# Eight one-bank PSUM tiles in place of four two-bank tiles, in a fused attention and mixer kernel

## The chip, the cores and the metric

The kernel runs on one core of one Trainium2 chip. The metric is the device time of one execution in microseconds (us); of several runs the median counts. A core has TensorE (PE, matrix products; its weight loads are the rows PEld), VectorE (DVE), ScalarE (ACT), GpSimd (POOL) and SyncE (SP, which here issues most DMAs). PE writes its results to PSUM, a memory of eight banks; a bank holds 512 float32 numbers in each of 128 partitions. DVE and ACT read the results from there.

## The reference

The shapes are B=8, H=8, S=576, D=64, so C=H*D=512; the token layer is 256 wide, the channel layer 1536.

```python
cum = np.cumsum(np.log(np.clip(f, 0.0001, 1.0)), axis=-1)
scores = q @ k.T / 8 + cum[..., :, None] - cum[..., None, :]
scores = np.where(causal, -1e9, scores)
attn = softmax(scores)                  # + 1e-9 in the denominator
x = (attn @ v) as (B, S, H*D)
u = x + (np.maximum(x.T @ w_tok1, 0) @ w_tok2).T
out = u + np.maximum(u @ w_ch1, 0) @ w_ch2
```

## The kernel before

The 64 heads of attention are worked in 32 pairs, four to each of the eight batch images. The two heads of a pair (s = 0 and 1) sit on the two halves of PE's rows. Products keep float32 accuracy by splitting an operand into a high and a low part, so that most products are three matmuls: high by high, high by low, low by high.

For a pair, the steps are these. POOL splits q and k (`hl`, L729 and L510). PE makes the scores of five row tiles t = 0 to 4, 64 to 576 columns wide because the mask is causal (`score`, L765). DVE adds the mask, writes the sum to SBUF (`pr`) and takes the minimum of each row, all in one custom instruction, followed by a short one that reads the minimum out into `nmin` (`rmin`, L775). ACT takes the exponential (`expo`, L779). DVE sums and inverts the denominators (L799, L802), and POOL scales (`norm`, L807). PE transposes the probabilities in three groups (`trs`, L825), two banks each; ACT copies the high part to `pt` (L504) and DVE subtracts for the low part (L513). PE multiplies with v (L870, and L858 for the low parts of the last piece), and ACT and DVE carry the result to `xt` (L885, L889). When an image is done, `mixer` runs on it piece by piece among the next pairs: transposes (L1353), products with the token weights and with the first 256 of the 1536 channels (`joint`, L1336), and what carries them out of PSUM (L504, L513, L516, L1416, L1465). That is the attention stage, up to 736 us. From 776 us a second stage runs the rest of the channel layer (L1152 to L1219), with weights that come by DMA.

The order of the work isn't that of the loops. The loops only create operations (`p.op(engine, duration, function, rd=..., wr=..., bufs=...)`). The class `Plan` then gives them out by the table `ORDER`, which holds for every engine the numbers of its operations in the order in which they are issued, and assigns each `Buf` a slot, among them the eight PSUM banks b0 to b7. The plan treats each bank as a resource of its own. In the program, however, PSUM is declared as four tiles `unit0` to `unit3` of 1024 columns (L1536), and a bank is the half of one (L1538): b0 and b1 are unit0, b2 and b3 unit1, b4 and b5 unit2, b6 and b7 unit3. The waits between the engines are set when the program is built, from the tiles that its instructions read and write.

The only buffer that uses a whole unit is the widest score tile, t = 4: 576 columns, as 288 and 288 columns on both sides of the bank border, read by one minimum of 576 columns. Its slot is of the kind "un" (L1477), a pair of banks. The other four score tiles of a head share two banks.

Of the kernel before, what the change touches and what calls it, by code (L numbers as in the profile page):

```python
# [9 lines left out]
F32 = mybir.dt.float32  # L10
F32R = mybir.dt.float32r
# [7 lines left out]
    FILL=36, F1=2, FQ=4, n_raw=1, n_vr=1, n_hl=1, n_vv=2, n_pr=2, n_pt=4, n_xn=1,  # L19
# [46 lines left out]
    ),  # L66
    DVE=(
# [390 lines left out]
def build(nc, env, dims):  # L458
# [261 lines left out]
    for n2 in range(HB // 2):  # L720
# [60 lines left out]
        for ts in ((4,), (3, 0), (2, 1)):  # L781
# [4 lines left out]
            for s in (0, 1):  # L786
                sm = (2 * n2 + s) % 4
                for t in ts:
                    p.op("DVE", d_dve(end[t]), lambda t=t, s=s, sm=sm, f=rmin: f(t, s, sm), rd=[ps[s]], wr=[(pr, s, t), ("nmin", sm, t)], bufs=[ps[s], pr])
# [914 lines left out]
```

## Time and profile before

| | |
|---|---|
| median of 3 runs | 1294.0 us (1290.93 to 1298.85) |
| the profiled execution, its own time | 1291.14 us |
| its span in the trace | 1289.4 us |
| PE busy | 1080.4 us, 84% of the span, 10030 matmuls |
| DVE busy | 862.2 us, 67%, 2093 instructions |
| ACT busy | 637.2 us, 49%, 1582 instructions |
| POOL busy | 440.2 us, 34%, 519 instructions |
| mean granted clock of PE | 0.939 of full speed |

Busy time is time in which an engine executes; the rest of the span it waits or issues. "Idle before" of an instruction is the time that its engine stood still just ahead of it, and the releaser is the instruction that ended last among those it waited for. A matmul's duration depends on the clock that PE is granted.

### The profile page before, as it was taken

Reading aid. Unit: us, or ns where it says so; the run is one execution under the profiler, and the core shown is the slowest. Engines: PE = TensorE matmul, PEld = TensorE weight load, DVE = VectorE, ACT = ScalarE, POOL = GpSimd, SP = SyncE. Lnnn points to the kernel's source line nnn. Section 1 sums busy time; section 2 is a strip of 40 time slices with the busy share of each in tenths; the row PEclk is TensorE's granted clock in tenths of the full one; section 3 lists DMA queues with packets and bytes.
Section 4 is the critical chain, followed back from the end, with each engine's and each line's share of the span. In section 5 each row is a group of like instructions: output and inputs, shape, how many; then the busy total and the mean of one; then the engine's idle time right before and its main releaser. Section 6 shows DMA issues by size and latency. Waiting matters only on the chain.

```text
span 1289.4 us, 26886 instructions
## 1 busy us (share of the span) xinstructions
PE 1080.4 (84%) x10030; PEld 935.8 (73%) x10030; DVE 862.2 (67%) x2093; ACT 637.2 (49%) x1582; POOL 440.2 (34%) x519
## 2 busy tenths in 40 slices
PE   6777887878877777778778779899999999899897
PEld 4566777877767677767667667778787787688776
DVE  7788565666464465465465687886797696588376
ACT  5577575666564556566566544333252252143132
POOL 6665546466454374465355200000211101110110
PEclk8678997999988989999999979999999999999999
DMA  6221221121312112121222257898979888877774
GB/s 196 86 61 56 70 75 51 48 97 33 117 42 93 60 62 84 29 75 38 74 84 73 73 190 259 264 312 258 314 233 303 265 249 276 267 239 216 263 233 155
DMA packets 125858, 192.77 MB, mean 150 GB/s; under 512 B 18976, under 2 KB 77088, under 8 KB 124704
## 3 DMA queue, kind: packets, MB, share of 16 engines
q1 hardware_dynamic: 125632, 190.91, 46.3%
q8 instruction: 79, 1.29, 0.4%
q14 instruction: 51, 0.42, 0.1%
q10 hardware_dynamic: 96, 0.15, 0.0%
HBM read 144.34 MB, written 46.66 MB: 148 GB/s over the span
## 4 chain that ended last, share of the span: by engine, by line
PE 46%; DVE 11%; ACT 7%; issue 4%; DMA 2%; SPq 0%; POOL 0%; DVEq 0%; ACTq 0%; POOLq 0%
PE unit L1336 8%; PE unit L1217 4%; PE unit L1219 4%; PE unit L1152 4%; PE unit L1218 4%; PE unit L1154 4%; PE unit L1153 4%; PE unit L870 3%; PE unit L765 3%; ACT pt L504 2%; DVE pt L513 2%; PE unit L825 1%; DVE xt L889 1%; DVE pr L775 1%; ACT pr L779 1%
## 5 line engine op out<-in xcount | busy, mean ns | idle before, releaser
L807 POOL TENSOR_SCALAR pr<-pr,rec 128x320 f32<-128x320 f32 (+4 forms) x320 | 166.8, 539 | 188.8 <-DVE rec L802 135.9
L779 ACT ACTIVATE pr<-pr,nmin 128x320 f32<-128x320 f32 (+4 forms) x320 | 177.2, 558 | 42.8 <-DVE nmin L775 42.1
L513 DVE TENSOR_TENSOR pt<-unit,pt 128x512 fp32r<-128x512 f32 x192 | 126.1, 685 | 91.4 <-ACT pt L504 55.1
L775 DVE CUSTOM_DVE_ANT_0 pr<-unit,mask 128x576 f32<-128x576 f32 (+4 forms) x320 | 145.8, 483 | 53.1 <-PE unit L765 19.4
L504 ACT ACTIVATE pt<-unit 128x512 fp32r<-128x512 f32 x192 | 106.0, 598 | 89.2 <-PE unit L1336 35.5
L870 PE MATMUL unit<-pt,vv 64*128 64x512 f32 (+7 forms) x1152 | 131.0, 350 | 22.0 <-DVE pt L513 9.9
L765 PE MATMUL unit<-hl 64*128 64x288 f32 (+4 forms) x1008 | 112.5, 318 | 34.5 <-DVE pt L513 14.1
L870 PEld LDWEIGHTS unit<-pt,vv 64*128 64x128 f32 x1152 | 109.6, 206 | 31.9 <-DVE pt L513 12.0
L765 PEld LDWEIGHTS unit<-hl 64*128 64x128 f32 x1008 | 92.7, 197 | 44.7 <-DVE pt L513 15.8
L825 PE MATMUL unit<-ident,pr 64*128 64x64 f32 x1536 | 74.5, 241 | 43.7 <-DVE nmin L775 15.0
L825 PEld LDWEIGHTS unit<-ident,pr 64*128 64x128 f32 x1536 | 65.0, 152 | 53.8 <-issue 12.8
L889 DVE TENSOR_TENSOR xt<-unit,xt 64x64 f32<-64x64 f32 (+1 forms) x128 | 57.5, 453 | 59.8 <-ACT xt L885 42.6
L885 ACT ACTIVATE xt<-unit 64x64 f32<-64x64 f32 (+1 forms) x128 | 50.6, 404 | 63.1 <-PE unit L870 28.0
L1336 PE MATMUL unit<-t2h,ring 64*128 64x288 f32 x512 | 66.6, 316 | 14.2 <-DVE xt L889 6.0
L765 PE MATMUL unit<-cd,sel 64*128 64x288 f32 (+4 forms) x384 | 77.9, 357 | 0.0
L1336 PE MATMUL unit<-ring,w2h 64*128 64x288 f32 x512 | 67.6, 312 | 12.1 <-DVE ring L516 3.9
L510 POOL TENSOR_TENSOR hl<-raw,hl 128x1152 fp32r<-128x1152 f32 x28 | 74.5, 2662 | 1.8
L1336 PE MATMUL unit<-xn,t1h 64*128 64x256 f32 x512 | 64.4, 321 | 11.0 <-DVE pt L513 5.7
L504 ACT ACTIVATE hid<-h 128x480 fp32r<-128x480 f32 x75 | 45.1, 603 | 54.7 <-PE unit L1218 33.6
L1336 PEld LDWEIGHTS unit<-t2h,ring 64*128 64x128 f32 x512 | 53.8, 198 | 21.4 <-DVE xt L889 8.4
L1170 ACT ACTIVATE h<-unit 128x480 f32<-128x480 f32 x20 | 11.3, 570 | 113.3 <-PE unit L1154 86.6
L1336 PEld LDWEIGHTS unit<-ring,w2h 64*128 64x128 f32 x512 | 53.2, 192 | 18.0 <-ACT ring L504 3.5
(246 smaller groups left out, 3076.7 us busy)
## 6 DMA issues: line engine op xcount, KB each, us to landing
pw<-wd SPq DMA_DIRECT2D x280, 256.0 KB, 3.9
raw<-in_qk SPq DMA_DIRECT2D x28, 576.0 KB, 4.0
d_raw<-in_w_ch SPq DMA_DIRECT2D x80, 128.0 KB, 3.1
ud<-xt SPq DMA_DIRECT2D x8, 1152.0 KB, 5.0
pd<-part SPq DMA_DIRECT2D x32, 288.0 KB, 2.5
wd<-pw SPq DMA_DIRECT2D x20, 384.0 KB, 4.3
vr<-in_v SPq DMA_DIRECT2D x64, 80.0 KB, 2.4
out_t<-d_raw SPq DMA_DIRECT2D x19, 240.0 KB, 3.7
```

Source lines behind the costliest of these rows:

```text
L504: nc.scalar.activation(out, in_, func, scale=scale)
L510: nc.gpsimd.tensor_tensor(out, in_, asf(hi), op=ALU.subtract)
L513: nc.vector.tensor_tensor(out, in_, asf(hi), op=ALU.subtract)
L765: nc.tensor.matmul(at(buf)[:, of : of + w], q, k, start=(x == 0), stop=(x == len(passes)))
L775: nc.vector.tensor_tensor_reduce(prob(t, s), x, y, -1.0 / D**0.5, 3e38, op0=ALU.add, op1=ALU.min, accum_out=E["nmin"][sm][:m, t : t + 1])
L779: nc.scalar.activation(x, x, AF.Exp, bias=E["nmin"][sm][:m, t : t + 1], scale=-1.0, accum_out=E["sums"][sm][:m, t : t + 1])
L807: nc.gpsimd.tensor_scalar(x, x, E["rec"][sm][:m, t // 2, t % 2 : t % 2 + 1], 0.0, op0=ALU.mult, op1=ALU.add)
L825: nc.tensor.transpose(at(ps[s])[:, k * D : (k + 1) * D], at(pr)[r, x, :, :].rearrange("p a b -> p (a b)"), E["ident"][r, r])
L870: nc.tensor.matmul(at(av[s])[:, 512 - w :], at(vv)[r, vblk(j), :], at(pt)[r, z, c : c + w], start=(z, gi, i) == (0, 0, 0), stop=(z, gi, i) ...
L889: "DVE", d_dve(n), lambda ps=ps, o=o, n=n, f=f, xt=xt, me=me, pp=pp: nc.vector.tensor_tensor(at(xt)[me, pp, o : o + n], at(ps)[me, f : f + ...
L1152: nc.tensor.matmul(o, wt[:, 0, :], h_, start=(first and k == 0), stop=False, skip_group_check=True)
L1336: last[s] = nc.tensor.matmul(at(ps[s ^ z])[:, : width[0]], a, m, start=(z == 0 and i == 0), stop=(z == 1 and i == len(todo[s]) - 1), skip_ ...
```

## The change

Four things change.

- PSUM is declared as eight tiles `bank0` to `bank7` of 512 columns.
- The widest score tile is split: columns 0 to 319 (t = 4) lie in one bank and 320 to 575 (t = 5) in another; they are two operations on PE and two minima on DVE. The first minimum goes to a spare column of `nmin`; the second starts from it (`first`) and so yields the minimum of the whole row. The exponential stays one instruction over 576 columns and follows the second minimum.
- `n_hl` goes from 1 to 2, in place of a second slot of `hl` that was laid over the weight buffer `d_raw`; `n_pt` goes from 4 to 3. `nmin` gets one column more.
- `ORDER` is new throughout, for 5357 operations instead of 5261 (32 more on PE, 64 more on DVE). The number of matmuls on PE stays.

```diff
-    FILL=36, F1=2, FQ=4, n_raw=1, n_vr=1, n_hl=1, n_vv=2, n_pr=2, n_pt=4, n_xn=1,
+    FILL=36, F1=2, FQ=4, n_raw=1, n_vr=1, n_hl=2, n_vv=2, n_pr=2, n_pt=3, n_xn=1,
...
-        "10:29 189 194 203 39:2 264 41:2 273 43:3 259 226 231 236 241 371 362 242:2 296 301 306 311:2 432 313 322 357 "
...
         for s in (0, 1):
-            c2, a, bb = Buf("un"), Buf("bk"), Buf("bk")
+            a, bb, c, d = (Buf("bk") for _ in range(4))
             where.append({
...
-                4: (c2, [(512 - HS, 0, HS), (512, HS, HS)]),
+                4: (c, 0, 0, end[2]),
+                5: (d, 0, end[2], end[4] - end[2]),
             })
...
-            nc.vector.tensor_tensor_reduce(prob(t, s), x, y, -1.0 / D**0.5, 3e38, op0=ALU.add, op1=ALU.min, accum_out=E["nmin"][sm][:m, t : t + 1])
+            o = at(pr)[:m, boff[z] + j0 // D : boff[z] + (j0 + w) // D, s, :]
+            first = 3e38 if t < 5 else c0[:m, NS : NS + 1]
+            col = NS if t == 4 else z
+            nc.vector.tensor_tensor_reduce(o, x, y, -1.0 / D**0.5, first, op0=ALU.add, op1=ALU.min, accum_out=c0[:m, col : col + 1])
...
-        for ts in ((4,), (3, 0), (2, 1)):
+        for ts in ((4,), (5,), (3, 0), (2, 1)):
...
-    pairs = [(f"b{2 * i}", f"b{2 * i + 1}") for i in range(4)]
-    k["un"] = pairs[::-1]
...
-    k["hl"].append(tuple(u for s in k["d_raw"] for u in s))
...
-    units = [psum.tile([P, 1024], F32, name=f"unit{i}") for i in range(4)]
-    E["un"] = {(f"b{2 * i}", f"b{2 * i + 1}"): x for i, x in enumerate(units)}
-    bank = {(f"b{i}",): units[i // 2][:, (i % 2) * 512 : (i % 2) * 512 + 512] for i in range(8)}
+    bank = {(f"b{i}",): psum.tile([P, 512], F32, name=f"bank{i}") for i in range(8)}
...
-    for nm, shape in (("nmin", [P, NS]), ("sums", [P, NS + 1]), ("rec", [P, NS // 2 + 1, 4])):
+    for nm, shape in (("nmin", [P, NS + 1]), ("sums", [P, NS + 1]), ("rec", [P, NS // 2 + 1, 4])):
```

The lines of the changed kernel lie 3 to 13 further down: the scores are at L768, the minima at L782, the exponential at L786, the transposes at L838, the copies at L508 and L517, `joint` at L1349.

How the new table moves instructions is shown at three places. A row is line, operation, what it writes <- what it reads, and the shape; in brackets the engines whose semaphores it waits for. The number behind a tile's name tells tiles apart.

The first is PE in the middle of the attention stage, before: the end of the second group of transposes of a pair, the start of the first half of the token layer for the image before, and the start of its second half.

```order
L825 MATMUL unit2_65<-ident_67,pr0_173 128x64
L825 MATMUL unit3_66<-ident_67,pr0_173 128x64
L1336 MATMUL unit1_64<-xn0_181,t1h_102 128x256 [waits DVE_49]
L1336 MATMUL unit3_66<-xn0_181,t1h_102 128x256 [waits DVE_49]
...
L1336 MATMUL unit3_66<-xn0_181,t1h_102 128x256 [waits PE_49,Activation_49]
L1336 MATMUL unit1_64<-xn0_181,t1h_102 128x256 [waits DVE_49]
L1336 MATMUL unit3_66<-xn0_181,t1l_103 128x256
```

The same place in the changed kernel:

```order
L838 MATMUL bank0_63<-ident_71,pr0_178 128x64
L838 MATMUL bank1_64<-ident_71,pr0_178 128x64
L1349 MATMUL bank2_65<-xn0_185,t1h_106 128x256 [waits DVE_49,Activation_49]
L1349 MATMUL bank6_69<-xn0_185,t1h_106 128x256 [waits DVE_49]
...
L1349 MATMUL bank6_69<-xn0_185,t1h_106 128x256 [waits PE_49]
L1349 MATMUL bank2_65<-xn0_185,t1h_106 128x256
L1349 MATMUL bank6_69<-xn0_185,t1l_107 128x256
```

The steps follow each other as before. Before, the transposes and the token layer both wrote halves of unit3; now their tiles have nothing in common, and the second half of the layer begins with no wait for ACT or DVE.

The second place is ACT just behind this, before: the copies of the transposes to `pt` among exponentials of the next pair.

```order
L779 ACTIVATE pr1_174,sums3_84<-pr1_174,nmin3_80 128x7x64
L504 ACTIVATE pt0_177<-unit2_65 128x8x64 [waits DVE_49,PE_49]
L504 ACTIVATE pt1_178<-unit3_66 128x8x64 [waits DVE_49,PE_49,Activation_49]
L779 ACTIVATE pr1_174,sums2_83<-pr1_174,nmin2_79 64x64
L504 ACTIVATE pt0_177<-unit1_64 128x8x64 [waits PE_49]
```

And in the changed kernel:

```order
L786 ACTIVATE pr1_179,sums3_88<-pr1_179,nmin3_84 128x7x64 [waits DVE_49,Activation_49]
L508 ACTIVATE pt0_182<-bank1_64 128x8x64 [waits DVE_49,PE_49,Activation_49]
L786 ACTIVATE pr1_179,sums2_87<-pr1_179,nmin2_83 128x9x64
L508 ACTIVATE pt0_182<-bank0_63 128x8x64 [waits Activation_49]
L508 ACTIVATE pt1_183<-bank7_70 128x8x64 [waits DVE_49,PE_49,Activation_49]
```

The copies come in the same order among the exponentials, but the second copy of a `pt` buffer no longer waits for PE.

The third place is DVE at the minima of the first pair, before:

```order
L775 ISA pr0_173,nmin1_78<-unit2_65,mask_72 128x9x64 [waits PE_49]
L775 ISA nmin1_78 128x1
L775 ISA pr0_173,nmin0_77<-unit3_66,mask_72 128x9x64
L775 ISA nmin0_77 128x1
L775 ISA pr0_173,nmin1_78<-unit0_63,mask_72 128x7x64 [waits PE_49]
```

And in the changed kernel:

```order
L782 ISA pr0_178,nmin0_81<-bank0_63,mask_76 128x5x64 [waits PE_49]
L782 ISA nmin0_81 128x1
L782 ISA pr0_178,nmin1_82<-bank1_64,mask_76 128x5x64 [waits PE_49]
L782 ISA nmin1_82 128x1
L782 ISA pr0_178,nmin0_81<-bank2_65,mask_76,nmin0_81 128x4x64 [waits DVE_49,PE_49]
```

Two pairs of instructions (one for each head, the second instruction of a pair being the read-out) have become four, and the later ones wait for PE and for the read-out before.

## Rows read from the trace of the kernel before

**Rows 1.** Windows: length, busy PE, PEld, DVE, ACT, POOL; PEclk, DMA share, GB/s

```profile
0.00:96.00 96.00, 67.67 (x609) 55.03 (x611) 74.21 (x207) 57.97 (x153) 62.18 (x89) 0.73 0.37 115
96.00:736.00 640.00, 510.39 (x6928) 463.61 (x6925) 375.94 (x1137) 388.84 (x1075) 325.02 (x391) 0.94 0.21 67
736.00:776.00 40.00, 28.71 (x309) 25.82 (x307) 35.35 (x79) 19.74 (x41) 4.56 (x4) 0.83 0.54 176
776.00:1289.00 513.00, 473.65 (x2194) 391.34 (x2193) 376.65 (x673) 170.69 (x314) 48.42 (x36) 0.98 0.81 256
```

**Rows 2.** Two stretches of the attention stage in the same view

```profile
224.00:352.00 128.00, 106.58 (x1549) 98.67 (x1547) 78.20 (x240) 83.44 (x233) 70.92 (x87) 0.99 0.23 74
352.00:480.00 128.00, 98.83 (x1272) 89.14 (x1268) 71.50 (x220) 73.58 (x201) 63.57 (x78) 0.89 0.19 63
```

**Rows 3.** Groups by line, 96 to 736 us: busy, mean ns, idle before, its releasers

```profile
L504 ACT ACTIVATE pt<-unit 128x512 fp32r<-128x512 f32 x174 | 96.1, 598 | 79.6 <-PE unit L1336 35.5 <-PE unit L825 14.6 <-DVE pt L513 11.9
L885 ACT ACTIVATE xt<-unit 64x64 f32<-64x64 f32 (+1 forms) x116 | 45.8, 404 | 54.8 <-PE unit L870 22.1 <-PE unit L1336 14.4 <-PE unit L765 9.8
L513 DVE TENSOR_TENSOR pt<-unit,pt 128x512 fp32r<-128x512 f32 x174 | 114.4, 685 | 84.6 <-ACT pt L504 52.1 <-PE unit L1336 20.9 <-PE unit L858 4.7
L775 DVE CUSTOM_DVE_ANT_0 pr<-unit,mask 128x576 f32<-128x576 f32 (+4 forms) x280 | 127.4, 483 | 47.0 <-PE unit L1336 17.0 <-PE unit L765 16.1 <-PE unit L825 5.0
L889 DVE TENSOR_TENSOR xt<-unit,xt 64x512 f32<-64x512 f32 (+1 forms) x116 | 52.2, 453 | 59.0 <-ACT xt L885 42.0 <-PE unit L1336 9.8 <-PE unit L765 5.8
```

**Rows 4.** Timeline of PE, 381 to 388 us: start, length, instruction, [idle before]

```profile
381.25 1.46 PE L825 MATMUL unit<-ident,pr 64*128 64x64 f32 x32
382.95 0.70 PE L1336 MATMUL unit<-xn,t1h 64*128 64x256 f32 x2 [0.23 <-DVE xn L513]
...
384.81 0.28 PE L1336 MATMUL unit<-ring,t1l 64*128 64x256 f32 x1
...
387.35 0.38 PE L1336 MATMUL unit<-xn,t1h 64*128 64x256 f32 x1 [1.15 <-DVE pt L513]
```

**Rows 5.** Timeline of ACT, the same stretch

```profile
382.70 0.60 ACT L504 ACTIVATE pt<-unit 128x512 fp32r<-128x512 f32 x1 [0.66 <-PE unit L825]
385.17 0.60 ACT L504 ACTIVATE pt<-unit 128x512 fp32r<-128x512 f32 x1 [1.87 <-PE unit L1336]
...
385.99 0.58 ACT L504 ACTIVATE pt<-unit 128x512 fp32r<-128x512 f32 x1
```

**Rows 6.** Timeline of DVE, the same stretch

```profile
383.24 0.36 DVE L775 CUSTOM_DVE_ANT_0 pr<-unit,mask 128x192 f32<-128x192 f32 x1
...
383.52 0.48 DVE L775 CUSTOM_DVE_ANT_0 pr<-unit,mask 128x320 f32<-128x320 f32 x1
...
383.94 0.69 DVE L513 TENSOR_TENSOR pt<-unit,pt 128x512 fp32r<-128x512 f32 x1
...
386.60 0.69 DVE L513 TENSOR_TENSOR pt<-unit,pt 128x512 fp32r<-128x512 f32 x1 [1.58 <-ACT pt L504]
```

**Rows 7.** What PE waited for, 96 to 736 us: total us, times, longest

```profile
PE unit L765 <- DVE pt L513: 14.1, 10, 2.4
PE unit L825 <- DVE nmin L775: 12.4, 14, 1.7
...
PE unit L825 <- POOL hl L729: 1.2, 2, 0.9
```

**Rows 8.** Chain of waits, 96 to 736 us, by line, shares of the whole span

```profile
by line: PE unit L1336 12.8%; PE unit L870 6.8%; PE unit L765 5.3%; ACT pt L504 3.6%; issue 3.3%; DVE pt L513 3.2%; PE unit L825 2.7%; DVE pr L775 2.4%; DVE xt L889 2.3%; ACT pr L779 2.2%; ACT xt L885 2.2%; ACT ring L504 1.4%; DVE xn L513 0
```

**Rows 9.** DVE's groups by shape, 96 to 736 us

```profile
L775 DVE CUSTOM_DVE_ANT_0 pr<-unit,mask 128x576 f32<-128x576 f32 x56 | 41.1, 750 | 3.2 <-PE unit L765 2.4 <-PE unit L858 0.6
L775 DVE CUSTOM_DVE_ANT_0 pr<-unit,mask 128x320 f32<-128x320 f32 x56 | 26.7, 485 | 11.7 <-PE unit L1336 3.9 <-PE unit L825 3.5 <-PE unit L765 2.6
L775 DVE CUSTOM_DVE_ANT_0 pr<-unit,mask 128x192 f32<-128x192 f32 x56 | 19.3, 351 | 4.9 <-PE unit L870 1.8 <-PE unit L1336 1.7 <-PE unit L765 0.7
L775 DVE DVE_READ_ACCUMULATOR2_ANT nmin<- 128x1 f32 x224 | 18.3, 82 | 0.0
```

More of the change, by code (lines that the diff above doesn't have):

```diff
@@ L741, in build @@
         for s in (0, 1):
-            c2, a, bb = Buf("un"), Buf("bk"), Buf("bk")
+            a, bb, c, d = (Buf("bk") for _ in range(4))
             where.append({
-                3: (a, [(0, 0, end[3])]),
-                0: (a, [(end[3], 0, end[0])]),
-                2: (bb, [(0, 0, end[2])]),
-                1: (bb, [(end[2], 0, end[1])]),
-                4: (c2, [(512 - HS, 0, HS), (512, HS, HS)]),
+                3: (a, 0, 0, end[3]),
+                0: (a, end[3], 0, end[0]),
+                2: (bb, 0, 0, end[2]),
+                1: (bb, end[2], 0, end[1]),
+                4: (c, 0, 0, end[2]),
+                5: (d, 0, end[2], end[4] - end[2]),
@@ L749, in build @@
             })
         def score(t, where=where, src=src, fq=fq, n2=n2):
-            i0 = start[t]
-            for g in range(len(where[0][t][1])):
-                passes = ((0, 1),) if fq else ((0, 1), (0, 3), (2, 1))
-                for x in range(len(passes) + 1):
-                    for s in (0, 1):
-                        buf, segs = where[s][t]
-                        of, j0, w = segs[g]
-                        rows = HALF[s]
-                        if x < len(passes):
-                            q, k = (at(src)[rows, y, :] for y in passes[x])
-                            q, k = q[:, i0 : i0 + P], k[:, j0 : j0 + w]
-                        else:
-                            q, k = E["sel"][rows, n2 : n2 + 1].to_broadcast([D, P]), E["cd"][rows, j0 : j0 + w]
-                        nc.tensor.matmul(at(buf)[:, of : of + w], q, k, start=(x == 0), stop=(x == len(passes)))
+            i0 = start[min(t, 4)]
@@ new lines, in score @@
+            passes = ((0, 1),) if fq else ((0, 1), (0, 3), (2, 1))
+            for x in range(len(passes) + 1):
+                for s in (0, 1):
+                    buf, of, j0, w = where[s][t]
+                    rows = HALF[s]
+                    if x < len(passes):
+                        q, k = (at(src)[rows, y, :] for y in passes[x])
+                        q, k = q[:, i0 : i0 + P], k[:, j0 : j0 + w]
+                    else:
+                        q, k = E["sel"][rows, n2 : n2 + 1].to_broadcast([D, P]), E["cd"][rows, j0 : j0 + w]
+                    nc.tensor.matmul(at(buf)[:, of : of + w], q, k, start=(x == 0), stop=(x == len(passes)))
@@ L767, in prob, with rmin @@
         def prob(t, s, pr=pr):
             return at(pr)[: size[t], boff[t] : boff[t] + end[t] // D, s, :]
-        def rmin(t, s, sm, where=where, prob=prob):
-            buf, segs = where[s][t]
-            m, of, w = size[t], segs[0][0], end[t]
-            a = S - P - start[t]
-            x, y = (z.rearrange("p (a b) -> p a b", b=D) for z in (at(buf)[:m, of : of + w], E["mask"][:m, a : a + w]))
-            nc.vector.tensor_tensor_reduce(prob(t, s), x, y, -1.0 / D**0.5, 3e38, op0=ALU.add, op1=ALU.min, accum_out=E["nmin"][sm][:m, t : t + 1])
+        def rmin(t, s, sm, where=where, pr=pr):
+            buf, of, j0, w = where[s][t]
+            z = min(t, 4)
+            m, c0 = size[z], E["nmin"][sm]
+            a = S - P - start[z] + j0
+            x, y = (v.rearrange("p (a b) -> p a b", b=D) for v in (at(buf)[:m, of : of + w], E["mask"][:m, a : a + w]))
+            o = at(pr)[:m, boff[z] + j0 // D : boff[z] + (j0 + w) // D, s, :]
+            first = 3e38 if t < 5 else c0[:m, NS : NS + 1]
+            col = NS if t == 4 else z
+            nc.vector.tensor_tensor_reduce(o, x, y, -1.0 / D**0.5, first, op0=ALU.add, op1=ALU.min, accum_out=c0[:m, col : col + 1])
@@ L779, in expo @@
             nc.scalar.activation(x, x, AF.Exp, bias=E["nmin"][sm][:m, t : t + 1], scale=-1.0, accum_out=E["sums"][sm][:m, t : t + 1])
-        for ts in ((4,), (3, 0), (2, 1)):
+        for ts in ((4,), (5,), (3, 0), (2, 1)):
             ps = [where[s][ts[0]][0] for s in (0, 1)]
-            dur = [hm(w, z) for t in ts for _, _, w in where[0][t][1] for z in ((4, 1) if fq else (1, 1, 1, 1))]
+            dur = [hm(where[0][t][3], z) for t in ts for z in ((4, 1) if fq else (1, 1, 1, 1))]
             rd = [raw, "cd"] if fq else [(hl, 0), (hl, 1), "cd"]
@@ L788, in build @@
                 for t in ts:
-                    p.op("DVE", d_dve(end[t]), lambda t=t, s=s, sm=sm, f=rmin: f(t, s, sm), rd=[ps[s]], wr=[(pr, s, t), ("nmin", sm, t)], bufs=[ps[s], pr])
+                    p.op(
+                        "DVE", d_dve(where[0][t][3]), lambda t=t, s=s, sm=sm, f=rmin: f(t, s, sm), rd=[ps[s]] + ([("nmin", sm, NS)] if t == 5 else []),
+                        wr=[(pr, s, t), ("nmin", sm, NS if t == 4 else min(t, 4))], bufs=[ps[s], pr],
+                    )
                 for t in ts:
+                    if t == 4:
+                        continue
+                    z = min(t, 4)
                     p.op(
-                        "ACT", d_act(end[t], False, 2), lambda t=t, s=s, sm=sm, f=expo: f(t, s, sm),
-                        rd=[("nmin", sm, t)], wr=[(pr, s, t), ("sums", sm, t)], bufs=[pr],
+                        "ACT", d_act(end[z], False, 2), lambda t=z, s=s, sm=sm, f=expo: f(t, s, sm),
+                        rd=[("nmin", sm, z)] + [(pr, s, 4)] * (t == 5), wr=[(pr, s, z), (pr, s, t), ("sums", sm, z)], bufs=[pr],
                     )
@@ L1605, in attn_mixer_kernel @@
         E[kind] = {((kind, i, 0), (kind, i, 1)): x for ((_, i),), x in E[kind].items()}
-    words = raws.rearrange("p i a b -> p (i a b)")[:, : 4 * S].bitcast(F32R)
-    E["hl"][tuple(u for x in E["d_raw"] for u in x)] = words.rearrange("p (k s) -> p k s", s=S)
     E["rr"] = {}
```

453 rows, old and new, of tables (ACT, DVE, PE, POOL) are left out of this document.

## The prediction

> **What bounds the kernel now.** The windows by stage come first [rows 1]. [...] In the steady attention stage (96 to 736 us) no engine is full: PE is busy 510.39 of 640 us at 0.94, ACT 388.84, DVE 375.94, POOL 325.02, and the DMA share is 0.21. Engines wait for each other there. PE's idle time is 640 - 510.4 = 129.6 us, and its work would take 510.4 x 0.94 = 479.8 us at the full clock, so at most 640 - 479.8 = 160.2 us can be won in this stage. It isn't an even loss: from 224 to 352 us PE got 106.58 us of work at 0.99 through in 128 us, which is 0.824 of a full engine, but from 352 to 480 us only 98.83 x 0.89 / 128 = 0.687 [rows 2]. The clock is low where PE was less busy.
>
> Next, what the waits are for [rows 3]. The releaser of an instruction should be the producer of what it reads. A copy to `pt` reads transposes (L825); a copy to `xt` reads products with v (L870, L858); a minimum reads scores (L765). But ACT's copies to `pt` stood 35.5 us for `joint` (L1336), which they do not read, and 14.6 us for the transposes, which they do. Copies to `xt` on ACT: 14.4 + 9.8 us for L1336 and L765, 22.1 us for L870. On DVE, the low parts of `pt`: 20.9 + 4.7 us for L1336 and L858; minima: 17.0 + 5.0 us for L1336 and L825 against 16.1 us for the scores; `xt`: 9.8 + 5.8 us for L1336 and L765. Together 35.5 + 14.4 + 9.8 + 20.9 + 4.7 + 17.0 + 5.0 + 9.8 + 5.8 = 122.9 us for matmuls of other data, against 14.6 + 22.1 + 16.1 = 52.8 us for the right ones: 70% of the time in which these five groups stood released by PE.
>
> The timeline shows how. The transposes of the second group end at 381.25 + 1.46 = 382.71 us [rows 4]. ACT could copy them when its copy of 382.70 is over, at 383.30, but starts at 385.17, released by L1336 [rows 5]. By the order of before the copied bank is in unit3, and the token layer that runs from 382.95 to 384.81 + 0.28 = 385.09 us writes the other bank of unit3: the wait is kept by unit. DVE, after 1.58 us idle, starts its subtraction of a bank of unit1 at 386.60, because ACT's copy ahead of it began only at 385.99 [rows 5, 6]; and PE's next half of the token layer, which writes the other bank of unit1, stands for that subtraction and starts at 387.35 after 1.15 us idle [rows 4]. Each wait has made the next one.
>
> **The change, part by part.**
>
> *One tile for each bank.* All waits on the other bank of a unit go; true ones (a bank to be filled before it is read, and read before it is filled again) stay. What it gives lies between 0 and 160.2 us of the attention stage; a loss can come only from the new order, and the rivals price it. Two nearer bounds: if the whole stage ran like its stretch 224 to 352 us it would take 479.8 / 0.824 = 582 us, 58 us less, and that stretch still holds such waits; if PE's idle time held the same 70% as ACT's and DVE's, 0.7 x 129.6 = 91 us would go. I take a quarter of the way from the first, which is measured, to the second, which supposes that nothing else is late next: -66 us. Late next is the true reuse of banks through DVE: PE waited 14.1 us with scores for subtractions of `pt` and 12.4 us with transposes for minima [rows 7], and a part of these is real. In the second stage PE's idle time is 39.4 us, all that could go; I take 0, with 10 us (a quarter of it) either way for the new order. The 96 us ahead of the stage and the 40 us behind it have DVE busy 74.21 and 35.35 us [rows 1] and prices of their own: 0, with 5 us either way.
>
> *The split minimum.* Durations for 192, 320 and 576 columns are 351, 485 and 750 ns [rows 9]; 256 columns lie midway between the first two, so 418 ns. A head pays 485 + 418 - 750 + 82 for one more read-out = 235 ns, 64 heads 15.0 us of DVE: the upper price. In the timeline, though, the step from one start to the next is shorter than a duration: 383.52 - 383.24 = 0.28 us for 192 columns, 383.94 - 383.52 = 0.42 us for 320, each with its read-out [rows 6]. That is 0.14 us for 128 columns, which leaves 0.28 - 192 x 0.14 / 128 = 0.07 us of fixed cost: 64 x 0.07 = 4.5 us is the lower price. On the path lies less: minima are 2.4% of the span on the chain, 31 us [rows 8], of 127.4 us [rows 3] and the read-outs' 18.3 us [rows 9], about a fifth. I take 15.0 / 5 = +3 us, between 1 and 15. DVE has room: 376 + 15 of 640 us.
>
> [...]
>
> *Scores, second slot of `hl`, third of `pt`.* PE writes 320 + 256 columns where it wrote 288 + 288, with as many matmuls: 0. The score banks of a pair stay eight. Two slots of `hl` let POOL split earlier: transposes waited 1.2 us for POOL's split [rows 7]; between 0 and 1.2 us, I take -1. The order of before names only `pt0` to `pt2`, so three slots are what there was: 0. DMAs keep their number, in a stage with a share of 0.21: 0.
>
> **Sum.** 1291.1 (the profiled execution) - 66 + 3 - 1 = 1227.1 us. The median of the runs shown is 2.9 us above the profiled one (1294.0 against 1291.1), so the forecast is **1230 us**.
>
> **The rivals.**
>
> *Other waits take the place.* Each instruction released sooner runs into its true wait (`<-ACT pt` 52.1 us and `<-ACT xt` 42.0 us are the largest rows of DVE's own, [rows 3], and these are no waits on a sibling bank). If half of the 58 us is so lost: 1291.1 - 29 + 3 + 2.9 = 1268 us. Against it: ACT itself stood longest for the wrong matmuls.
>
> *It goes further.* The clock is at 0.99 where PE is busiest [rows 2]; fewer gaps could bring it to full speed throughout, worth 510.4 - 479.8 = 30.6 us. Then 70% of 160.2 us go: 1291.1 - 112 + 3 - 1 + 2.9 = 1184 us. Against it: POOL, ACT and DVE hold 325 to 389 us each of true work, in chains.
>
> *Slower: the chained minimum.* The exponential of the widest tile now follows two minima and two read-outs. If DVE's queue is what each pair waits for, all 15.0 us lie on the path; and if the waits removed only covered true ones, nothing is won against it: 1291.1 + 15.0 + 2.9 = 1309 us. It decides as soon as DVE sets the pace of a pair; for that its stage total of 391 us would have to become the longest queue, and PE's 480 us stand against it. [...]
>
> *It does not do what it says.* The new order could place as much true reuse as the old had false: then only the minimum's price is left, 1291.1 + 3 + 2.9 = 1297 us. Against it: in the order rows the second half of the token layer has lost its wait for DVE.
>
> **How the numbers follow.** About 1% (13 us) is what a measurement of this kernel can tell from no change. Chances: the forecast 0.68, its own range 1205 to 1255; other waits 0.16; further 0.06; no effect 0.05; the chained minimum 0.05. Faster by over 1% means below 1281 us: the forecast, the rival "further" and most of "other waits" (0.13), 0.87; within 1%: the rest of "other waits" and "no effect", 0.08; slower 0.05. The range 1187 to 1274 leaves out half of "further" (0.03), some 0.06 of "other waits", and the last two (0.10).
>
> **What would show each step right or wrong.** In the changed kernel's rows ACT's and DVE's waits for L1349 at `pt`, `xt` and the minima should nearly vanish. The attention stage should end some 65 us sooner, PE's idle time in it fall by half, and its clock stand near 0.97. Minima should be 384, with the 256-column form near 418 ns. The second stage should still take about 513 us. The forecast fails if DVE's waits for ACT, or PE's for DVE at the reuse of a bank, grow by what the others lose; or if POOL's scaling, now asked for sooner, makes transposes wait.

## The result: 1044.8 us, a fifth less, and the profile after

The changed kernel takes 1044.8 us (median of 4 runs, 1043.7 to 1045.4) against 1292.5 us: a ratio of 0.808, 95% interval 0.805 to 0.811. The forecast had the direction and the mechanism, but a quarter of the size: 1230 us, range 1187 to 1274.

The windows, with the same columns as [rows 1], cut at about the same places in the work. The profiled execution took 1044.65 us, its span is 1042.9 us:

```profile
0.00:96.00 96.00, 69.39 (x715) 56.99 (x716) 85.82 (x247) 65.26 (x170) 67.40 (x92) 0.79 0.36 115
96.00:540.00 444.00, 432.31 (x6777) 421.88 (x6775) 367.90 (x1221) 372.53 (x1053) 321.40 (x388) 0.98 0.29 95
540.00:570.00 30.00, 22.00 (x245) 19.08 (x244) 27.23 (x56) 14.62 (x31) 6.13 (x4) 0.80 0.55 178
570.00:1043.00 473.00, 465.27 (x2304) 397.03 (x2302) 385.48 (x701) 177.52 (x331) 46.32 (x36) 1.00 0.87 284
```

Nearly as many matmuls as in the 640 us before (6777 against 6928) now take 444 us, and PE is idle for 11.7 us of them instead of 129.6. Its busy time fell too, from 510.39 to 432.31 us. The second stage went from 513 to 473 us, though this cut leaves 110 matmuls more in it.

Cut exactly at the last transposes of the mixer, which end the attention stage (742.0 and 549.0 us, rows further down), before and then changed:

```profile
96.00:742.00 646.00, 513.39 (x6970) 466.09 (x6967) 381.80 (x1151) 391.89 (x1082) 326.73 (x392) 0.94 0.21 67
96.00:549.00 453.00, 438.07 (x6864) 427.08 (x6863) 376.84 (x1238) 379.43 (x1067) 323.62 (x390) 0.98 0.29 94
```

With the 609 and 715 matmuls of the first 96 us, both have 7579 matmuls behind them. From the start, busy time falls from 581.1 to 507.5 us (74 us) and idle time from 160.9 to 41.5 us (119 us): the 193 us that this stage loses.

The groups of [rows 3] in the attention stage of the changed kernel, 96 to 540 us:

```profile
L517 DVE TENSOR_TENSOR pt<-bank,pt 128x512 fp32r<-128x512 f32 x166 | 107.8, 683 | 16.3 <-ACT pt L508 15.4
L782 DVE CUSTOM_DVE_ANT_0 pr<-bank,mask 64x64 f32<-64x64 f32 (+3 forms) x272 | 105.6, 426 | 5.5 <-PE bank L768 4.9
L508 ACT ACTIVATE pt<-bank 128x512 fp32r<-128x512 f32 x167 | 91.2, 597 | 16.9 <-PE bank L838 12.2 <-ACT pr L786 1.3 <-ACT part L1478 1.3
L902 DVE TENSOR_TENSOR xt<-bank,xt 64x512 f32<-64x512 f32 (+1 forms) x114 | 50.6, 449 | 22.5 <-ACT xt L898 20.7
L898 ACT ACTIVATE xt<-bank 64x64 f32<-64x64 f32 (+1 forms) x113 | 44.1, 403 | 11.8 <-PE bank L883 9.3 <-DVE xt L902 0.2
```

The durations of the copies and subtractions are those of before (the mean of the minima is over other forms; the 256-column form has a row of its own, shown further down). The waits are not: the largest wait of every group is now for the producer of what it reads, and no row names `joint` (now L1349). ACT's copies to `pt` stand 16.9 us instead of 79.6, the minima 5.5 and, in the 256-column form, 1.8 instead of 47.0.

The place of [rows 4] and [rows 5], the token layer of the fourth image, in the changed kernel: PE first, then ACT.

```profile
302.00 0.65 PE L838 MATMUL bank<-ident,pr 64*128 64x64 f32 x16
302.47 0.64 PE L1349 MATMUL bank<-xn,t1h 64*128 64x256 f32 x2
...
304.37 1.16 PE L838 MATMUL bank<-ident,pr 64*128 64x64 f32 x32
305.34 0.37 PE L1349 MATMUL bank<-xn,t1h 64*128 64x256 f32 x2
```

```profile
302.75 0.60 ACT L508 ACTIVATE pt<-bank 128x512 fp32r<-128x512 f32 x1
303.24 0.77 ACT L786 ACTIVATE pr<-pr,nmin 128x576 f32<-128x576 f32 x1
...
304.00 0.59 ACT L508 ACTIVATE pt<-bank 128x512 fp32r<-128x512 f32 x1
305.15 1.57 ACT L508 ACTIVATE pt<-bank 128x512 fp32r<-128x512 f32 x3 [0.56 <-ACT pt L508]
```

The first group of transposes ends at 302.65; ACT copies one of their banks from 302.75 and the other from 304.00, in the middle of the token layer, which it waited out before. PE goes from the transposes to the layer's second half with no idle time ahead of the row at 305.34; before, that place cost 1.15 us. (The new order has put the second group of transposes behind the layer's first half.)

What PE still waits for in this stage, the largest two rows, to be held against [rows 7], and the chain of waits, against [rows 8]. The shares in both are of the window asked for (here 444 us, there 640 us), not of the span as the heading of [rows 8] has it; and the chain before reaches back only to 392.75 us, so its rows cover 343 of the 640 us.

```profile
PE bank L768 <- DVE nmin L782: 2.7, 7, 1.0
PE bank L883 <- DVE pt L517: 2.3, 1, 2.3
```

```profile
by line: PE bank L1349 38.0%; PE bank L883 17.0%; PE bank L768 15.7%; PE bank L838 8.2%; DVE pr L782 3.6%; ACT pr L786 2.6%; DVE xt L902 2.2%; ACT xt L898 2.1%; PE bank L1366 1.4%; DVE pt L517 1.3%; issue 1.3%; DVE xn L517 1.2%; DVE d_g L59
```

PE is 80% of the chain; the largest pieces between are DVE's minima and ACT's exponentials.

### The profile page after: what moved, and what is told of

The parts are those of the page before. It is cut to its first block, busy times and chain, and to the rows that moved or that the text cites. A ratio compares the mean times of both kernels' runs of the same rounds, so it can differ in the third digit from the quotient of the medians.

```text
span 1042.9 us, 26969 instructions
## 1 busy us (share of the span) xinstructions
PE 989.0 (95%) x10030; PEld 895.0 (86%) x10030; DVE 866.4 (83%) x2221; ACT 629.9 (60%) x1582; POOL 441.3 (42%) x519
## 4 chain that ended last, share of the span: by engine, by line
PE 78%; DVE 14%; ACT 4%; DMA 2%; issue 1%; POOL 0%; SPq 0%; DVEq 0%; ACTq 0%
PE bank L1349 18%; PE bank L883 8%; PE bank L768 7%; PE bank L1165 6%; PE bank L1166 6%; PE bank L1167 6%; PE bank L1232 6%; PE bank L1230 6%; PE bank L1231 6%; PE bank L838 4%; DVE pr L782 3%; DVE xt L902 2%; DVE d_g L592 1%; ACT pr L786 1%; DVE pt L517 1%
## 5 line engine op out<-in xcount | busy, mean ns | idle before, releaser
L820 POOL TENSOR_SCALAR pr<-pr,rec 128x576 f32<-128x576 f32 (+4 forms) x320 | 169.8, 551 | 104.6 <-DVE rec L815 85.3
L786 ACT ACTIVATE pr<-pr,nmin 64x64 f32<-64x64 f32 (+4 forms) x320 | 177.2, 559 | 19.2 <-DVE nmin L782 18.6
L517 DVE TENSOR_TENSOR pt<-bank,pt 128x512 fp32r<-128x512 f32 x192 | 124.8, 682 | 16.4 <-ACT pt L508 15.4
L782 DVE CUSTOM_DVE_ANT_0 pr<-bank,mask 128x320 f32<-128x320 f32 (+3 forms) x320 | 124.8, 426 | 5.6 <-PE bank L768 4.9
L883 PE MATMUL bank<-pt,vv 64*128 64x512 f32 (+7 forms) x1152 | 115.6, 335 | 4.6 <-DVE pt L517 4.5
L508 ACT ACTIVATE pt<-bank 128x512 fp32r<-128x512 f32 x192 | 105.2, 597 | 19.8 <-PE bank L838 14.5
L768 PE MATMUL bank<-hl 64*128 64x320 f32 (+4 forms) x1008 | 105.5, 307 | 5.0 <-DVE nmin L782 3.7
L883 PEld LDWEIGHTS bank<-pt,vv 64*128 64x128 f32 x1152 | 102.4, 197 | 7.2 <-DVE pt L517 6.1
L768 PEld LDWEIGHTS bank<-hl 64*128 64x128 f32 x1008 | 87.4, 188 | 8.8 <-DVE nmin L782 5.4
L838 PE MATMUL bank<-ident,pr 64*128 64x64 f32 x1536 | 70.8, 232 | 14.7 <-DVE nmin L782 6.4
L838 PEld LDWEIGHTS bank<-ident,pr 64*128 64x128 f32 x1536 | 64.1, 145 | 17.4 <-POOL pr L820 14.9
L508 ACT ACTIVATE hid<-h 128x480 fp32r<-128x480 f32 x77 | 45.8, 602 | 54.1 <-PE bank L1231 36.9
L768 PE MATMUL bank<-cd,sel 64*128 64x320 f32 (+4 forms) x384 | 74.0, 340 | 4.1 <-DVE cd L551 4.1
L902 DVE TENSOR_TENSOR xt<-bank,xt 64x512 f32<-64x512 f32 (+1 forms) x128 | 57.2, 453 | 24.3 <-ACT xt L898 21.7
L1349 PE MATMUL bank<-xn,t1h 64*128 64x256 f32 x512 | 63.6, 313 | 2.9 <-DVE ring L517 1.9
L786 ACT ACTIVATION_READ_ACCUMULATOR pr<-pr,nmin 128x1 f32 (+1 forms) x320 | 62.6, 196 | 0.0
L1349 PE MATMUL bank<-ring,w2h 64*128 64x288 f32 x512 | 59.9, 297 | 1.6 <-DVE ring L520 1.5
L1349 PE MATMUL bank<-ring,w1h 64*128 64x288 f32 x512 | 59.5, 305 | 1.3 <-POOL ring L514 1.3
L508 ACT ACTIVATE ring<-xt 128x576 fp32r<-128x576 f32 (+3 forms) x64 | 39.3, 632 | 34.5 <-DVE xt L1429 19.4
```

What stands on the lines that cost most here:

```text
L508: nc.scalar.activation(out, in_, func, scale=scale)
L517: nc.vector.tensor_tensor(out, in_, asf(hi), op=ALU.subtract)
L768: nc.tensor.matmul(at(buf)[:, of : of + w], q, k, start=(x == 0), stop=(x == len(passes)))
L782: nc.vector.tensor_tensor_reduce(o, x, y, -1.0 / D**0.5, first, op0=ALU.add, op1=ALU.min, accum_out=c0[:m, col : col + 1])
L786: nc.scalar.activation(x, x, AF.Exp, bias=E["nmin"][sm][:m, t : t + 1], scale=-1.0, accum_out=E["sums"][sm][:m, t : t + 1])
L820: nc.gpsimd.tensor_scalar(x, x, E["rec"][sm][:m, t // 2, t % 2 : t % 2 + 1], 0.0, op0=ALU.mult, op1=ALU.add)
```

## The experiments

Theory 1: the waits on the other bank of a two-bank tile were the loss, and the declaration alone gives the time. Theory 2: the new order gives it. Medians in us; the ratio is to the kernel before in the same set of runs.

| kernel | order | PSUM tiles | median | ratio, interval |
|---|---|---|---|---|
| before | old | 4 x 2 banks | 1290 to 1294 | |
| old order, minimum split | old | 4 x 2 | 1304.6 | 1.008 (1.005 to 1.012) |
| old order, eight tiles | old | 8 x 1 | 1066.1 | 0.825 (0.819 to 0.831) |
| old order, eight tiles, free banks | old | 8 x 1 | 1065.8 | 0.824 (0.819 to 0.829) |
| new order, four tiles | new | 4 x 2 | 1308.6 | 1.012 (1.005 to 1.018) |
| new order, half and half | new | 4 x 1, 2 x 2 | 1158.4 | 0.896 (0.892 to 0.899) |
| changed | new | 8 x 1 | 1044.8 | 0.808 (0.805 to 0.811) |

**Old order, eight tiles.** The order table of before stays; one operation issues both minima.

```diff
-    units = [psum.tile([P, 1024], F32, name=f"unit{i}") for i in range(4)]
...
+    bank = {(f"b{i}",): psum.tile([P, 512], F32, name=f"bank{i}") for i in range(8)}
...
-                4: (c2, [(512 - HS, 0, HS), (512, HS, HS)]),
+                4: (c2, [(512 - end[2], 0, end[2]), (512, end[2], end[4] - end[2])]),
...
+                for of, j0, w in segs:
...
```

> The kernel before with its own order of work, but with PSUM declared as eight one-bank tiles; the widest score tile stays in a pair of banks (320 columns in one, 256 in the other) and its minimum is two chained instructions inside one operation. Theory 1 (the waits on the other bank of a unit were the loss, the new order is secondary): about 1060 us, between 1045 and 1110; PE idle in the attention stage falls from 130 us below 40. Theory 2 (the new order gives the time): 1280 to 1300 us. Theory 3 (each gives about half): about 1170 us.

1066.1 us: theory 1. Three of the same groups in its attention stage (its lines are L510, L519 and L900):

```profile
L519 DVE TENSOR_TENSOR pt<-bank,pt 128x512 fp32r<-128x512 f32 x172 | 111.7, 683 | 15.7 <-ACT pt L510 14.9
L510 ACT ACTIVATE pt<-bank 128x512 fp32r<-128x512 f32 x174 | 95.3, 597 | 23.6 <-PE bank L840 17.5 <-DVE xt L1431 2.5 <-ACT pr L794 1.4
L900 ACT ACTIVATE xt<-bank 64x512 f32<-64x512 f32 (+1 forms) x113 | 44.3, 402 | 13.9 <-PE bank L885 7.3 <-PE bank L873 2.8 <-DVE xt L904 1.8
```

With not one step of the order changed, no row of these names `joint` here either; nor do the other two groups, where the minima wait longest for the scores (5.8 us) and DVE's `xt` for ACT (18.1 us).

Where the time was in each kernel is read from two lines' first and last start: the transposes of the mixer, whose last ones end the attention stage, and the first product line of the long block of the second stage. Three kernels, each with its two rows (count: shortest/median/longest ns, first and last start us); the first is before, the second the old order on eight tiles, the third the changed one.

```profile
L1353 PE MATMUL unit<-ident,xt x320: 213/223/368, 68.8 to 742.0; 64*128 64x64 f32 x160
L1152 PE MATMUL unit<-ring,pw x120: 377/381/602, 879.6 to 1233.8; 128*128 128x480 f32 x120
```

```profile
L1368 PE MATMUL bank<-ident,xt x320: 213/223/367, 63.7 to 569.1; 64*128 64x64 f32 x160
L1167 PE MATMUL bank<-ring,pw x120: 377/381/383, 690.6 to 1013.7; 128*128 128x480 f32 x120
```

```profile
L1366 PE MATMUL bank<-ident,xt x320: 213/223/367, 63.6 to 549.0; 64*128 64x64 f32 x160
L1165 PE MATMUL bank<-ring,pw x120: 377/381/480, 665.3 to 989.9; 128*128 128x480 f32 x120
```

From before to eight tiles with the old order: the attention stage loses 742.0 - 569.1 = 172.9 us, the way from there to the block 137.6 - 121.5 = 16.1, the block 354.2 - 323.1 = 31.1, the tail 55.6 - 50.9 = 4.7; together 224.8 us of span. The new order, with what else the changed kernel has, takes off another 21.7 us, of which 569.1 - 549.0 = 20.1 in the attention stage.

The block of the second stage, in the same view as [rows 1], before and then with eight tiles:

```profile
880.00:1234.00 354.00, 330.97 (x1465) 273.29 (x1465) 250.96 (x406) 111.64 (x204) 41.60 (x31) 0.99 0.83 261
```

```profile
691.00:1014.00 323.00, 321.32 (x1465) 273.61 (x1464) 246.94 (x407) 112.42 (x205) 45.57 (x31) 1.00 0.90 287
```

1465 matmuls in the same order: PE's idle time falls from 23.0 to 1.7 us, its busy time by 9.7 us. The idle time was there to see in the trace of before, in the groups by line of that stage:

```profile
L1152 PE MATMUL unit<-w2l,pw 128*128 128x480 f32 x25 | 10.1, 405 | 2.7 <-DVE d_raw L1264 1.3 <-DVE h L1178 0.7 <-ACT h L1170 0.7
...
L1152 PE MATMUL unit<-t1h,pw 128*128 128x480 f32 x20 | 8.1, 407 | 1.4 <-DVE h L1173 1.3
```

Small pieces, spread over a dozen or more rows. These two start a product and wait for DVE or ACT to carry out a result; with one-bank tiles the view of PE's waits has 0.5 us left for this line, of 9.2 us for DVE and ACT before. Others (2.4 us of L1219, 2.5 of L1034) wait for the low part that they read, and 9.0 us ahead of L1152 the profile puts to no releaser. Which of them the declaration caused is not traced one by one; that it caused most is shown by the block above.

**New order, four tiles.**

```diff
-    bank = {(f"b{i}",): psum.tile([P, 512], F32, name=f"bank{i}") for i in range(8)}
+    units = [psum.tile([P, 1024], F32, name=f"unit{i}") for i in range(4)]
+    bank = {(f"b{i}",): units[i // 2][:, (i % 2) * 512 : (i % 2) * 512 + 512] for i in range(8)}
```

> The changed kernel with one edit: the banks are halves of four two-bank tiles again, the order and the split tile stay. Theory 1 (waits on the other bank): it goes back to about 1290 us, or above, since the new order was never bent around such waits. Theory 2 (the new order): 1045 to 1060 us. Theory 3: about 1170 us.

1308.6 us: one declaration, put back, costs 263.8 us, the whole gain of 247.7 and 16 more. Its window and two groups, 96 to 755 us:

```profile
96.00:755.00 659.00, 530.67 (x6764) 478.08 (x6762) 380.09 (x1230) 383.95 (x1050) 323.54 (x391) 0.89 0.20 64
```

```profile
L517 DVE TENSOR_TENSOR pt<-unit,pt 128x512 fp32r<-128x512 f32 x168 | 111.0, 685 | 82.9 <-ACT pt L508 45.9 <-PE unit L1349 14.8 <-PE unit L883 8.9
...
L508 ACT ACTIVATE pt<-unit 128x512 fp32r<-128x512 f32 x169 | 95.0, 596 | 103.1 <-PE unit L1349 40.1 <-DVE pt L517 17.6 <-PE unit L838 13.6
```

ACT's copies wait for `joint` again. And this pair of kernels shows what was wrong with the bound of the prediction: matmuls of one order, nearly as many (6764 and 6777 in the windows), keep PE busy 530.67 us at a granted clock of 0.89 here and 432.31 us at 0.98 in the changed kernel. Busy time shrinks with the stops, and the clock accounts for half of the 98 us: 530.67 x 0.89 = 472.3 against 432.31 x 0.98 = 423.7 us still differ by 49 us. How far the clock goes shows in the trace of before, where six 64x288 matmuls of L1336 take 0.72 us from 396.00 us (clock 0.55 from 395.0 to 398.8 us) and 0.39 us from 399.36 us (1.00 from 398.8 to 400.4). A matmul that runs alone shows 0.38 us [rows 4]; in a stream, 48 of the same line take 3.18 us, 0.066 us each, as this piece of the changed kernel's chain (start, length) shows:

```profile
185.62 3.18 PE bank L1349 x48
```

So a stop can add some tenths of a microsecond that the views count as busy. An estimate bears this out: over the 7579 matmuls up to the mixer's last transposes, the view of PE's waits, summed over its rows, has 182 stops before (0 to 742 us, clock 0.91) and 41 in the changed kernel (0 to 549 us, 0.95), and 581.05 x 0.91 - 507.45 x 0.95 = 46.7 us over the 141 more are 0.33 us each, beside 0.38 - 0.066 = 0.31.

The weight loads (PEld) move less with the stops. Their busy time times the clock is 478.08 x 0.89 = 425.5 us here and 421.88 x 0.98 = 413.4 in the changed kernel, 12 us apart where PE's are 49 apart. For the kernel before, PEld in [rows 1] gives 463.61 x 0.94 = 435.8 us, so a ceiling of 640 - 435.8 = 204 us, an estimate after the fact; 640 - 444 = 196 were won.

**Half and half.** Banks 0 to 3 as one-bank tiles, 4 to 7 as halves of two units, new order.

> The changed kernel with banks 0 to 3 as one-bank tiles and banks 4 to 7 as halves of two two-bank tiles. If each pair of banks brings its own waits and they add up, half of the 264 us between 1045 and 1309: about 1175 us. If the slack of the single banks takes up some of the waits, less than half: 1080 to 1140. If waits on two units already hold everything up, 1250 or more.

1158.4 us, 113.6 of the 263.8 us between 1044.8 and 1308.6: 43%, a little under half. That fits pairs of banks that bring their own waits, which nearly add up; the other half (banks 0 to 3 as halves) was not run. This kernel holds its own control, the same copies from both sorts of tile (window 96 to 700 us):

```profile
L508 ACT ACTIVATE pt<-bank 128x512 fp32r<-128x512 f32 x97 | 54.7, 596 | 11.6 <-PE bank L838 10.2 <-ACT pr L786 1.2
L508 ACT ACTIVATE pt<-unit 128x512 fp32r<-128x512 f32 x77 | 44.4, 597 | 40.4 <-PE unit L1349 8.8 <-DVE nmin L782 7.0 <-PE unit L768 5.7
```

0.12 us of idle time a copy from a single bank, nearly all for the transposes; 0.52 us from a unit, where the largest row (8.8 us) is for L1349's matmuls of other data and L838's transposes are not among the first three.

**Old order, only the minimum split.** The split of the first experiment, on four two-bank tiles.

> The kernel before with its order and its four two-bank tiles; only the minimum of the widest score tile is split in two chained instructions of 320 and 256 columns. It prices the split on the old path: +3 us by the prediction (1294 to 1298), up to +15 us if all of it lies on the path.

1304.6 us over ten runs against 1293.6 of thirteen: +11 us, interval +6 to +15 (0.46% to 1.17%). The split costs more than the +3 us of the prediction and lies within its two prices, nearer the upper one of 15. It also moves the comparison: from this kernel to the first one the declaration alone gives 1304.6 - 1066.1 = 238.5 us.

**The split in the changed kernel.** Two edits, each in a kernel of its own, price DVE's time there: the first minimum computed twice (the first line below), and the second one started from a constant (so that it leaves 320 columns out of the row's minimum).

```diff
+            for _ in range(2 if t == 4 else 1):
...
-            first = 3e38 if t < 5 else c0[:m, NS : NS + 1]
+            first = 3e38
```

> The changed kernel, with the first minimum (320 columns) of every widest score tile computed twice, 64 instructions of 0.42 to 0.57 us with their read-outs, some 30 us of DVE. If DVE, now 83% busy, sets the pace of the attention stage, +20 to +30 us (1065 to 1075); if the other engines' slack hides it, below +5 us (under 1050).

> The changed kernel with the second minimum of the widest score tile started from a constant instead of from the first one's result, so it leaves the first 320 columns out of the row's minimum. The 256-column form took 477 ns with the chained start value, where 418 ns was interpolated. If the start value from memory costs those 60 ns, and DVE's time counts one for one as with the doubled minimum, -4 us (1040 to 1041) and the form shows near 418 ns; if it is hidden, 1044 to 1046.

1072.9 us: +28.1 us for 64 x 0.42 = 26.9 us of DVE by the start-to-start step of [rows 6]. The last transposes of the mixer start at 575.9 us instead of 549.0, so all of it is in the attention stage. DVE's time counts one for one there, although it is busy 83% of the stage. 1040.4 us (1037.9 to 1041.8) without the chained start: -4.4 us between the medians, from different sets of runs; the changed kernel's single runs lie between 1039.2 and 1046.1. The form with 256 columns and its neighbours, in the changed kernel and then without the chain:

```profile
L782 DVE CUSTOM_DVE_ANT_0 pr<-bank,mask 128x320 f32<-128x320 f32 x109 | 51.2, 481 | 4.1 <-PE bank L768 3.6
...
L782 DVE CUSTOM_DVE_ANT_0 pr<-bank,mask,nmin 128x256 f32<-128x256 f32 x54 | 25.0, 477 | 1.8 <-PE bank L768 0.6 <-ACT ring L508 0.5
...
L782 DVE CUSTOM_DVE_ANT_0 pr<-bank,mask 128x192 f32<-128x192 f32 x55 | 18.6, 347 | 1.0 <-PE bank L768 1.0
```

```profile
L782 DVE CUSTOM_DVE_ANT_0 pr<-bank,mask 128x256 f32<-128x256 f32 x54 | 21.7, 416 | 1.1 <-PE bank L768 1.1
```

416 ns is close to the interpolated 418; the start value read from memory adds 61 ns, and 64 x 61 ns = 3.9 us.

**Free banks for the widest tile.** The old order on eight tiles, with any two free banks in place of a neighbouring pair.

> The old order on eight one-bank tiles, as in the run of 1066 us, but the widest score tile takes any two free banks instead of a neighbouring pair. Theory A (the 21 us that the old order lacks against the new come from the paired banks, which must both be free): about 1045 to 1050 us. Theory B (they come from the order of the operations itself): 1060 to 1070 us.

1065.8 us: no gain. So the 21 us between 1066 and 1045 are put to the order of the operations itself (theory B), with the banks that follow from it, since this run and the next one leave little else. Which of its moves gives them was not tried.

**One slot for the split q and k.** `n_hl=1` in the changed kernel takes the second slot away altogether (before, it lay over `d_raw`). Beside it ran the changed kernel unaltered on the same chip.

> The changed kernel with one slot for the split q and k instead of two; the order stays. The prediction gave the second slot 0 to 1.2 us. With PE now 95% busy a late split shows more: 10 of 28 pairs used the second slot, each may wait up to POOL's 2.7 us for one part, so between 0 and +27 us; the theory that POOL has slack: under +5 us.

> The changed kernel unaltered, beside the three other kernels of this set on the same chip: 1044 to 1046 us.

1046.1 us (1045.5 to 1046.9) against 1044.4 us (1042.2 to 1046.1): 1.7 us between the medians, with ranges that overlap. The second slot is worth about 2 us or nothing, near the 1.2 us that its row allowed, and not the 27 us that was also thought possible.

**A faster version: one DVE instruction less.** The sums of the exponentials are at least 1, where 1e-9 vanishes in float32, so the reciprocal can read them directly.

```diff
-                nc.vector.tensor_scalar(E["rec"][sm][:, :, :2], E["sums"][sm].rearrange("p (a b) -> p a b", b=3), 1e-9, None, op0=ALU.add)
...
-                nc.vector.reciprocal(E["rec"][sm][:, :, :2], E["rec"][sm][:, :, :2])
+                nc.vector.reciprocal(E["rec"][sm][:, :, :2], E["sums"][sm].rearrange("p (a b) -> p a b", b=2))
```

> The changed kernel without the DVE instruction that adds 1e-9 to the sums (64 of them, 0.15 us each by duration); the reciprocal reads the sums directly. The sums are at least 1, where the addend vanishes in float32. If DVE sets the pace of the attention stage, as the doubled minimum says, the start-to-start share of 64 instructions (0.09 us each) comes off: -6 us, to about 1039, at most -10 us. If only the chain through a minimum counts, nothing: 1044 to 1046.

> The changed kernel unaltered, in more rounds beside the version without the addition: 1044 to 1046 us.

> The version without the addition of 1e-9 to the sums, in more rounds, since four runs of each left the two ranges touching: 1039 to 1041 us, 4 us under the changed kernel, if the first look was right; no difference if it was scatter.

First 1040.4 us (1036.7 to 1043.1) beside 1044.4; then, in more rounds, 1039.9 us (1037.5 to 1041.0) beside 1044.5 (1039.2 to 1046.0). Both times 4 to 5 us, near the 6 expected, though single runs of the two overlap: a gain of 0.4% that the medians show twice, no more.

## Why the prediction was right or wrong

- *What bounds the kernel, and what the waits are for*: right for the attention stage. That 70% of the waits for PE in the five groups of [rows 3] were for matmuls of other data held, and the declaration alone, with the old order and the split, takes them out of these rows.
- *"At most 160.2 us can be won in this stage"*: **wrong, and the step that failed.** It took PE's busy time times the granted clock, 479.8 us, as work that has to stay. The stage lost 742.0 - 549.0 = 193 us, since busy time itself fell by 74 us where the bound allowed it 30.6 (510.4 - 479.8, the clock alone): PE's stops stretch what counts as busy, and busy time times the clock is 423.7 us in the changed kernel's window. The nearer bound of 58 us was made from the same quantity: the best stretch (0.824 of an engine) was taken for what the work allows, while it held the same waits as the rest. The other, 91 us, took ACT's and DVE's 70% for PE's idle time; in the window of [rows 1] that fell by 118 of 129.6 us, 91%.
- *-66 us for the tiles*: mis-sized by these bounds; measured -172.9 us with the old order (and the split) in the attention stage alone. "Late next is the true reuse of banks through DVE" was not what happened to PE: of 14.1 and 12.4 us in [rows 7] the largest rows left are 2.7 and 2.3. Nor did the 52.1 us of DVE's waits for ACT at `pt` stay, which the first rival took for true: they were 15.4 us afterwards, as ACT's own idle time ahead of these copies fell from 79.6 to 16.9 us.
- *The second stage, 0 with 10 us either way*: wrong. Its 39.4 us of idle time (513 - 473.65, [rows 1]) were taken for 0 without their groups being read as those of the attention stage were. The check of releaser against producer would have found a part; 9.0 us have no releaser in the profile. Eight tiles alone take 31 us from the long block and 16 from the way to it.
- *The split minimum, +3 us*: too small; the step that failed is the fifth taken of its price. On the old path it is +11 us. Its price there, by the steps from start to start, is 4.5 us and 3.9 more for the chained start value, whose 61 ns no row of before could show: 8.4 us, and 15.0 by the durations. So on the old path, too, about all of it counted, and in the changed kernel the doubled minimum says the same. The fifth was misread besides. By [rows 8] 2.4% of the window of 640 us are 15 us on the chain, not 31. But the chain covers only the window's last 343 us, in which minima and read-outs take 75.4 us, so that a fifth comes out by luck.
- *The second slot of `hl`, -1 us*: not told apart from 0 by what was measured (1.7 us, ranges that overlap). The third of `pt` was not tried by itself.
- *The rivals.* "It goes further" was the nearest, and its price (1184 us) still stopped at 70% of the false ceiling. "Slower", with 15 us on the path, is the +11 us of the split without the declaration: on two-bank tiles the one 576-column minimum is 11 us faster than the split one (1293.6 against 1304.6 us). No run here had it together with one-bank tiles.

## What to carry to other kernels

Check, for each costly group, whether the releaser in its row produces what the instruction reads; where it does not, ask which shared declaration ties the two together, in every stage and not only in the one that looks idle. A ceiling for the gain may not be taken from PE's busy time while PE stops often: nearly the same matmuls in the same order were busy 530.7 and 432.3 us. The weight loads' busy time times the clock was the steadier measure here (425.5 and 413.4 us). An engine's share of the chain is no price for an instruction added to it: about a fifth of the minima's time lay on the chain and DVE was busy 59% of the stage, yet the split cost about all of its time (+11 us for 8.4 to 15.0 us of DVE).

## What the hardware showed unexpectedly

A minimum over 256 columns on VectorE took 477 ns when its start value came from memory, 416 ns with a constant. PE's granted clock rose with the waits gone, from 0.94 to 0.98 of full speed in the attention stage, with nearly the same matmuls in fewer stops; with the new order on two-bank tiles it was 0.89. With PE idle for 128.3 us there against 11.7, that same order of matmuls also showed it busy for 98 us more (530.67 against 432.31 us).
